# Attention and feed-forward on one core: a second tile of six sequences, first products in halves, weight splitting on GpSimd

## The chip, the cores and the metric

One core of one Trainium2 chip. The metric is device time in microseconds of one execution. The engines are TensorE (PE, its weight loads PEld), VectorE (DVE), ScalarE (ACT), GpSimd (POOL) and SyncE (SP), which issues the transfers.

## What is computed

```python
B, H, S, D = (8, 8, 576, 64); stride = 32          # q, k, v in float32
scores = scale * np.matmul(q, k.transpose(0, 1, 3, 2))
mask_local = (rel >= 0) & (rel < stride)            # heads 0 to 3
mask_strided = (rel >= 0) & (pos[None, :] % stride == pos[:, None] % stride)   # heads 4 to 7
attn = softmax(np.where(masks, scores, -1e9))
x = np.matmul(attn, v).transpose(0, 2, 1, 3).reshape(B * S, H * D)    # 4608 x 512
h = x @ w_in                                        # 512 x 2048
g = 0.5 * h * (1.0 + erf(h * inv_sqrt2))
return g @ w_out                                    # 2048 x 512
```

## The kernel before

The 4608 tokens are taken in 12 tiles of 384. A tile is a list of 12 strided rows of 32 tokens; the table `VISITS` says in which order the rows (r0 to r1 of a sequence b) are taken. For each tile 16 feed-forward steps follow, one for each block of 128 hidden channels, 192 in all. Step n makes `H_n` (`ffn_h`, 12 first products of 384 columns, for four channel blocks c of x: c 0 and 1 come from the local heads, 2 and 3 from the strided ones), then gelu, a high part `gh` and a low part `gl` (`ffn_g`), and then adds to the output banks (`ffn_o`, 9 second products of 512 columns). Every operand is a pair of a high part and a low part, so that three products stand for one.

Attention lies between these steps. The local heads are "jobs" L0 to L35, three to a tile, whose scores and values are small products of TensorE. The strided heads are computed by VectorE, unit by unit (at most 4 rows of a visit), one multiply-and-sum of 64 channels for each pair of a row and an earlier row, and one accumulation for each pair again; only tile 0's strided heads go over TensorE (`half_tile` a and b, `strided_tile` A). Once a tile, at step 13 of the tile, `visit` issues the value products of the next tile's jobs and the scores of the tile after that, 144 small products in a row; below this is a tile change.

The weights come as packed 64-bit words, one load of 1 MB for each of 16 blocks (`load_w`, at most three on their way). `split_w` makes the pair of parts of a block f in five operations: `lead` (the top 16 bits, L154 or L156), the upper halves `other` (L159), a merge with a shift (L161), the high part (L165 or L167) and the low part (L169). These, the first three local jobs, tile 0's strided heads, steps 0 to 15 of the feed-forward (`f0` to `f15`) and the strided unit jobs of tile 1 (`u1`) are issued in an order written out by hand, the list `START`, one word for one piece of a job: `w` loads a weight, `c` splits it, `q` and `v` load a local job's inputs, `L` runs it, `S` and `B` load tile 0's strided inputs. Each engine runs its own instructions in this order. After it, `step` places the steps, the tile changes and the strided operations by a rule of shares.

Of the kernel before, what the change touches and what calls it, by code (L numbers as in the profile page):

```python
# [10 lines left out]
F32 = mybir.dt.float32  # L11
# [13 lines left out]
P = 128  # L25
# [13 lines left out]
VISITS = [(0, 0, 12), (1, 0, 4), (2, 0, 4), (3, 0, 4), (4, 0, 18), (5, 0, 18), (6, 0, 18), (7, 0, 18),  # L39
          (1, 4, 18), (2, 4, 18), (3, 4, 18), (0, 12, 18)]  # L40
# [8 lines left out]
    q0 q2 S0 q1 v0 w0 B0 w1 L0 w3 L2 L0 L0 L2 L2 L0 a0 L0 L0 b0 a0 L2 a0 L0 L2 a0 L1 L2 b0 b0 b0 L0 L1  # L49
    L2 a0 L0 b0 a0 L1 b0 a0 b0 w2 a0 b0 a0 q5 b0 L0 a0 v2 L1 L2 b0 L0 v1 c0 L1 a0 q4 L1 b0 c0 L1 A0 L1  # L50
    c0 A0 w5 A0 c1 c0 A0 c0 c1 A0 c3 L5 c1 c3 L2 L5 L1 c2 v5 c1 w6 L4 c3 w4 L1 L2 c2 L1 L2 L4 f0 L5 w7
    c2 L4 c1 c2 f0 f1 L5 c2 f0 c5 f0 L4 c5 f0 c3 f1 c5 f1 f2 c4 f1 c4 c5 c3 f1 f2 f2 c4 c7 L5 f2 c4 c5
    f3 L5 w8 c7 c4 w9 E f2 f3 L5 c6 f3 c7 c6 f4 f3 c7 c6 w12 f3 c7 f4 f4 c8 c6 f5 w10 f4 c8 v3 c6 q3 w11
    c9 c8 f4 f5 u1 f5 c9 f6 f5 w13 u1 c8 v4 c9 f5 c12 w15 c8 f6 e f6 f7 c12 u1 c9 f6 c12 f6 f7 f7 c9 w14
    c10 f8 f7 c12 u1 c10 c12 f7 f8 c10 c11 f9 u1 c11 c10 f8 c13 c11 L4 L3 f9 f8 f9 c10 f8 c13 f9 c11 c13
    f10 c14 c11 c14 L3 f9 c13 f10 c14 f10 L4 f11 u1 f10 c13 L3 f10 L4 u1 f11 L3 f12 u1 f11 c14 f11 u1
    f13 f12 f12 c15 c14 f11 f13 f12 f13 u1 c15 f14 f13 u1 f12 f14 c15 f14 f14 c15 L3 u1 f13 L3 c15 u1 L3
# [3 lines left out]
TOP_V = [6]  # L61
HIGH_V = [0, 1, 2, 3, 5, 6, 10, 13]
QUOT_V = (0, 1)
# [3 lines left out]
def units(most):  # L67

    res = []
    for k, (vi, b, r) in enumerate(ROWS):  # L70
        if res and res[-1][0] == vi and k % TR and res[-1][3] < most:
            res[-1][3] += 1
        else:
            res.append([vi, b, r, 1, k // TR, k % TR])
    return res
# [7 lines left out]
def attn_ffn_kernel(ctx: ExitStack, tc: tile.TileContext, qk, vl, qka, va, qs, ks, vs, w, out):  # L83
# [30 lines left out]
    smask = const.tile([P, MA], F32, name="smask")  # L114
    mask = const.tile([P, LK], F32, name="mask")
    mask0 = const.tile([P, LK], F32, name="mask0")

    bmask = {i: const.tile([P, 2 * STRIDE], F32, name=f"bmask{i}") for i in (None, 0, 1)}
# [22 lines left out]
    def split_w(f):  # L141
# [9 lines left out]
        lead = lpool.tile([P, 2 * DM], F16, name=f"lead_{f}", tag="lead", bufs=1)  # L151
# [7 lines left out]
        nc.scalar.activation(other.bitcast(I32), lead.bitcast(I16), AF.Copy, scale=65536.0)  # L159
# [11 lines left out]
        w2[f] = wt[:, :, DM:]  # L171

# [109 lines left out]
    def band_job(x, bt, sx=None):  # L282
# [25 lines left out]
        msk = bmask[first_[0] if first_ else None]  # L308
# [150 lines left out]
    def load_strided(gr, nm):  # L459

        if gr is None:
            return
        src = {"q": qs, "k": ks, "v": vs}[nm]
        t = spool.tile([P, NR, D], F32, name=f"s{nm}_{gr}", tag=f"s{nm}", bufs=1)
        for vi in first_of[gr]:
            b, r0, r1 = VISITS[vi]
            o = groups[vi][1]
            sq[vi, nm] = t[:, o:o + r1]
            if nm != "q":
                r0 = 0  # L470
            nc.sync.dma_start(t[:, o + r0:o + r1], src[b, :, r0:r1])
# [8 lines left out]
    def strided_qk(u):  # L480
        vi, _, r0, nr, t, k = PLACE[u]
        W = r0 + nr
# [7 lines left out]
        for c in range(W):  # L490
            for r in range(max(0, c - r0), nr):
                def f(r=r, c=c):
                    junk = spool.tile([P, D], F32, name=f"junk_{u}_{r}_{c}", tag="junk", bufs=4)
                    nc.vector.tensor_tensor_reduce(  # L494
                        junk, sq[vi, "q"][:, r0 + r, :], sq[vi, "k"][:, c, :], 1.0, 0.0,
                        ALU.mult, ALU.add, ss[u][:, r, c:c + 1])
                ops.append((0.137, f))
# [10 lines left out]
    def strided_av(u):  # L508
        vi, _, r0, nr, t, k = PLACE[u]
        W = r0 + nr  # L510
# [17 lines left out]
        for c in range(W):  # L528
            for r in range(max(0, c - r0), nr):
                def f(r=r, c=c):  # L530
                    acc = ss[u, "acc"]
                    wgt = ss[u][:, r, c:c + 1]
                    if c == 0:
                        nc.vector.tensor_scalar_mul(acc[:, r, :], sq[vi, "v"][:, c, :], wgt)
                    else:
                        nc.vector.scalar_tensor_tensor(  # L536
                            acc[:, r, :], sq[vi, "v"][:, c, :], wgt, acc[:, r, :], ALU.mult, ALU.add)
                ops.append((0.196, f))
# [16 lines left out]
    def alternate(us, what, first):  # L555
# [7 lines left out]
        for ops in zip(*todo):  # L563
# [4 lines left out]
            for u, x in zip(us, ops):  # L568
                r0, nr = PLACE[u][2:4]
                key = [r for c in range(r0 + nr) for r in range(max(0, c - r0), nr)]  # L570
                rows_ += [[f for k, f in zip(key, x) if k == r] for r in range(nr)]
# [377 lines left out]
```

## Time and profile before

| what | value |
|---|---|
| median of 3 runs | 876.04 us (874.67 to 878.77) |
| the profiled execution | 877.5 us, span 875.7 us |
| TensorE busy | 856.4 us of the span |
| VectorE, ScalarE, GpSimd busy | 706.2, 482.7, 17.5 us |
| transfers | 66.67 MB, 76 GB/s in the mean |

The span runs from the first to the last instruction. Busy times of TensorE are modelled, since products overlap; the distance from one product to the next says more than the length of one.

### The profile page before, as it was taken

What the parts mean: (1) busy time and instruction counts of PE and PEld (TensorE: products, weight loads), DVE (VectorE), ACT (ScalarE), POOL (GpSimd) and SP (SyncE); (2) the same over time, 40 slices, a digit from 0 to 9 for tenths busy, and PEclk for the clock granted to TensorE, in tenths of its full rate; (3) what the DMA queues carried; (4) which work ended last, traced back from release to release, by engine and by line L of the source; (5) the groups of instructions that cost most, each with busy time, mean ns of one, the idle gap of its engine ahead of it and who ended that gap; (6) DMA issues with size and microseconds to landing.
All of it is one profiled execution on the core that took longest, in us unless ns stands there. A gap on an engine that the chain in (4) does not pass through costs nothing.

```text
span 875.7 us, 19634 instructions
## 1 busy us (share of the span) xinstructions
PE 856.4 (98%) x6082; PEld 771.0 (88%) x6082; DVE 706.2 (81%) x4901; ACT 482.7 (55%) x1001; POOL 17.5 (2%) x89
## 2 busy tenths in 40 slices
PE   5999999999999999999999999999999989999998
PEld 4888898999999999999999899989989979989997
DVE  6998999998989997889999979899799993751111
ACT  7888585566465375357355445556547435443222
POOL 5000100000000000000000000000000000000000
PEclk9799999999999999999999999999999999999999
DMA  9695301320310320310311121131032002000001
GB/s 352 223 380 200 115 24 37 108 76 8 128 47 9 101 97 10 104 44 8 97 50 58 55 76 47 34 122 48 9 101 80 12 30 59 18 6 12 26 1 37
DMA packets 34552, 66.67 MB, mean 76 GB/s; under 512 B 6800, under 2 KB 16528, under 8 KB 34448
## 3 DMA queue, kind: packets, MB, share of 16 engines
q1 hardware_dynamic: 34448, 65.43, 22.1%
q8 instruction: 48, 0.79, 0.4%
q14 instruction: 56, 0.46, 0.2%
HBM read 51.64 MB, written 9.44 MB: 70 GB/s over the span
## 4 chain that ended last, share of the span: by engine, by line
PE 90%; DVE 3%; DMA 3%; ACT 2%; SPq 1%; issue 1%; DVEq 0%; ACTq 0%
PE H L619 15%; PE O L659 14%; PE O L660 14%; PE H L621 14%; PE H L620 14%; PE O L658 14%; PE X_L L337 1%; PE S L297 1%; DMA ws<-in_w_dram 1%; DMA qka<-in_qka_dram 1%; DMA sk<-in_ks_dram 1%; DVE ws L161 1%; SPq L326 1%; PE S L337 1%; DVE w L169 1%
## 5 line engine op out<-in xcount | busy, mean ns | idle before, releaser
L628 ACT ACTIVATE H<-H 128x384 f32<-128x384 f32 x192 | 91.3, 476 | 363.0 <-PE H L621 304.3
L619 PE MATMUL H<-xh,w 128*128 128x384 f32 x768 | 261.6, 341 | 1.5 <-DVE gl L632 1.4
L621 PE MATMUL H<-xh,w 128*128 128x384 f32 x768 | 260.6, 339 | 0.0
L620 PE MATMUL H<-xl,w 128*128 128x384 f32 x768 | 259.4, 338 | 0.4 <-DVE xl L238 0.4
L536 DVE SCALAR_TENSOR_TENSOR acc<-sv,sc,acc 128x64 f32<-128x64 f32 x1158 | 249.5, 275 | 0.7
L660 PE MATMUL O<-w,gl 128*128 128x512 f32 x576 | 228.3, 396 | 0.0
L659 PE MATMUL O<-w,gh 128*128 128x512 f32 x576 | 227.7, 395 | 0.0
L658 PE MATMUL O<-w,gh 128*128 128x512 f32 x576 | 224.4, 390 | 0.0
L494 DVE CUSTOM_DVE_ANT_0 junk<-sq,sk 128x64 f32<-128x64 f32 x1290 | 203.8, 217 | 3.5 <-DMA sk<-in_ks_dram 2.4
L632 DVE TENSOR_TENSOR gl<-H,gh 128x384 fp32r<-128x384 f32 x192 | 105.7, 551 | 106.0 <-ACT gh L630 105.1
L619 PEld LDWEIGHTS H<-xh,w 128*128 128x128 f32 x768 | 145.4, 189 | 11.1 <-DVE gl L632 1.7
L620 PEld LDWEIGHTS H<-xl,w 128*128 128x128 f32 x768 | 145.3, 189 | 8.5 <-DVE xl L238 0.8
L621 PEld LDWEIGHTS H<-xh,w 128*128 128x128 f32 x768 | 145.0, 189 | 0.1
L660 PEld LDWEIGHTS O<-w,gl 128*128 128x128 f32 x576 | 108.1, 188 | 23.7 <-DVE gl L632 0.6
L659 PEld LDWEIGHTS O<-w,gh 128*128 128x128 f32 x576 | 108.1, 188 | 18.2
L658 PEld LDWEIGHTS O<-w,gh 128*128 128x128 f32 x576 | 108.5, 188 | 17.3
L494 DVE DVE_READ_ACCUMULATOR2_ANT sc<- 128x1 f32 x1290 | 103.6, 80 | 0.0
L630 ACT CAST gh<-H 128x384 fp32r<-128x384 f32 x192 | 92.2, 480 | 6.1
L628 ACT ACT_TABLE_LOAD x60 | 77.0, 1283 | 1.0
L504 ACT ACT_TABLE_LOAD x35 | 44.9, 1283 | 0.6
L315 ACT ACTIVATE PT_L<-P_L,nm_L 128x64 f32<-128x64 f32 x132 | 44.2, 337 | 0.3
L315 ACT ACT_TABLE_LOAD x24 | 30.8, 1283 | 0.5
(114 smaller groups left out, 488.7 us busy)
## 6 DMA issues: line engine op xcount, KB each, us to landing
ws<-in_w_dram SPq DMA_DIRECT2D x16, 1023.8 KB, 10.1
qk<-in_qk_dram SPq DMA_DIRECT2D x36, 320.0 KB, 5.0
out_dram<-ob SPq DMA_DIRECT2D x34, 256.0 KB, 2.4
vl<-in_vl_dram SPq DMA_DIRECT2D x36, 192.0 KB, 4.3
sk<-in_ks_dram SPq DMA_DIRECT2D x8, 576.0 KB, 5.5
sv<-in_vs_dram SPq DMA_DIRECT2D x8, 576.0 KB, 3.9
band<-PT_L SPq DMA_DIRECT2D x240, 16.0 KB, 1.8
sq<-in_qs_dram SPq DMA_DIRECT2D x4, 576.0 KB, 4.4
```

Source lines behind the costliest of these rows:

```text
L315: nc.scalar.activation(pv[:, :, h, :], p1[:, h * 2 * QB:(h + 1) * 2 * QB].rearrange("p (c t) -> p c t", c=2), AF.Exp, bias=nm[:, h:h + 1], ...
L494: nc.vector.tensor_tensor_reduce(junk, sq[vi, "q"][:, r0 + r, :], sq[vi, "k"][:, c, :], 1.0, 0.0, ALU.mult, ALU.add, ss[u][:, r, c:c + 1])
L536: nc.vector.scalar_tensor_tensor(acc[:, r, :], sq[vi, "v"][:, c, :], wgt, acc[:, r, :], ALU.mult, ALU.add)
L619: nc.tensor.matmul(hp, w1[f][:, 0, c, :], xh[:, c, :], start=(c == 0), stop=False)
L620: nc.tensor.matmul(hp, w1[f][:, 0, c, :], xl[:, c, :], start=False, stop=False)
L621: nc.tensor.matmul(hp, w1[f][:, 1, c, :], xh[:, c, :], start=False, stop=(c == NC - 1))
L628: nc.scalar.activation(hp, hp, AF.Gelu)
L630: nc.scalar.copy(gh, hp)
L632: nc.vector.tensor_tensor(gl, hp, gh.bitcast(F32), ALU.subtract)
L658: nc.tensor.matmul(o, gh[:, sl], w2[f][:, 0, :], start=(f == 0), stop=False)
L659: nc.tensor.matmul(o, gh[:, sl], w2[f][:, 1, :], start=False, stop=False)
L660: nc.tensor.matmul(o, gl[:, sl], w2[f][:, 0, :], start=False, stop=(f == NF - 1))
```

## The change

The order of the rows is another: tile 1 now holds two rows of each of six sequences, and the rest of these sequences follows in one visit each. A unit may now hold rows of several sequences, and one load brings the six sequences. Steps 0 and 1 make their first products in two halves of the channel blocks; step 0 begins with the local half, step 1 with the strided half. Seven of the upper halves and eight of the high parts go to GpSimd. `lead` has two buffers. The lead-in products at the very start go from 49 to 28. Masks and zeros lie in the `pbig` buffer. The scores for tiles 4 and 9 are issued two steps after the tile change instead of in it. `START` is another list, and GpSimd's work in it is now in the written order too.

```diff
-VISITS = [(0, 0, 12), (1, 0, 4), (2, 0, 4), (3, 0, 4), (4, 0, 18), (5, 0, 18), (6, 0, 18), (7, 0, 18),
-          (1, 4, 18), (2, 4, 18), (3, 4, 18), (0, 12, 18)]
+VISITS = [(0, 0, 12), *[(b, 0, 2) for b in range(1, 7)], (7, 0, 18), *[(b, 2, 18) for b in range(1, 7)],
+          (0, 12, 18)]
...
-    q0 q2 S0 q1 v0 w0 B0 w1 L0 w3 L2 L0 L0 L2 L2 L0 a0 L0 L0 b0 a0 L2 a0 L0 L2 a0 L1 L2 b0 b0 b0 L0 L1
+    q2 q0 q1 S0 w0 w1 v2 v0 L2 B0 v1 L0 L2 w4 L1 L2 L0 L0 L1 L2 b0 L2 L1 L2 L0 a0 b0 L0 b0 L0 L1 b0 L1
...
-TOP_V = [6]
-HIGH_V = [0, 1, 2, 3, 5, 6, 10, 13]
-QUOT_V = (0, 1)
+TOP_V = [5, 6]
+HIGH_V = [2]
+
+WORD_P = [0, 4, 6, 8, 11, 12, 14]
+HIGH_P = [0, 1, 3, 4, 5, 6, 7, 8]
+QUOT_V = (1, 2)
+
+HALVES = {0: ((0, 1), (2, 3)), 1: ((2, 3), (0, 1))}
...
-        lead = lpool.tile([P, 2 * DM], F16, name=f"lead_{f}", tag="lead", bufs=1)
+        lead = lpool.tile([P, 2 * DM], F16, name=f"lead_{f}", tag="lead", bufs=2)
...
-        nc.scalar.activation(other.bitcast(I32), lead.bitcast(I16), AF.Copy, scale=65536.0)
+        if f in WORD_P:
+            nc.gpsimd.tensor_scalar(other.bitcast(I32), lead.bitcast(I16), 65536.0, None, ALU.mult)
+        else:
+            nc.scalar.activation(other.bitcast(I32), lead.bitcast(I16), AF.Copy, scale=65536.0)
...
+        elif f in HIGH_P:
+            nc.gpsimd.tensor_copy(wt[:, 0, :], hf)
...
-    def ffn_h(n):
+    def ffn_h(n, parts=None):
+
         t, f = divmod(n, NF)
         xh, xl = xt[t]
-        hp = ps_h.tile([P, TT], F32, name=f"H_{n}", tag="H")
-        for c in range(NC):
...
+        hp = hps[n] = ps_h.tile([P, TT], F32, name=f"H_{n}", tag="H")
+        parts = parts or (range(NC),)
+        for cs in parts:
+            for c in cs:
+                nc.tensor.matmul(hp, w1[f][:, 0, c, :], xh[:, c, :], start=(c == parts[0][0]), stop=False)
...
+            yield
...
-    for i in range(49):
+    for i in range(28):
...
-    with tc.manual_schedule(engines={ET.DVE, ET.Activation, ET.PE, ET.SP}):
+    with tc.manual_schedule(engines={ET.DVE, ET.Activation, ET.PE, ET.SP, ET.Pool}):
...
-    FIRST, VISIT = 2, 13
+    FIRST, VISIT, LATE = 2, 13, (4, 9)
...
-    score_at = {ready[1] + FIRST: 2, **{n: t + 1 for n, t in value_at.items()}}
+    score_at = {ready[1] + FIRST: 2, **{n + 2 * (t + 1 in LATE): t + 1 for n, t in value_at.items()}}
```

The written order decides what each engine does next. On VectorE, before, from the merge of weight block 0 (`ws_0`) to the maxima of job 5 (`xl_0` is the low part of tile 0's x, `w_0` the split weight):

```order
L161 SCALAR_TENSOR_TENSOR ws_0_305<-ws_0_305 128x1024
L435 STREAM_TRANSPOSE qka_0_297<-A0_0_357 128x256
...
L165 CAST w_0_596<-ws_0_305 128x1024
L169 TENSOR_TENSOR w_0_596<-ws_0_305,w_0_596 128x1024
L441 TENSOR_TENSOR xl_0_494<-qka_0_297,xh_0_493 128x4x48 x4
L161 SCALAR_TENSOR_TENSOR ws_1_308<-ws_1_308 128x1024
L311 ISA P_L5_638,nm_L5_640<-S0_1_610,bmask0_90 128x64
```

The same stretch of VectorE's list in the change:

```order
L174 SCALAR_TENSOR_TENSOR ws_0_281<-ws_0_281 128x1024
...
L433 TENSOR_TENSOR va_0_278<-va_0_278,Az_0_0_459 128x8x24
L261 TENSOR_TENSOR xl_0_505<-S0_L0_307,xh_0_504 128x2x128
...
L184 TENSOR_TENSOR w_0_492<-ws_0_281,w_0_492 128x1024
L261 TENSOR_TENSOR xl_0_505<-S0_L1_326,xh_0_504 128x2x128
L174 SCALAR_TENSOR_TENSOR ws_1_283<-ws_1_283 128x1024
L458 STREAM_TRANSPOSE qka_0_277<-A0_0_396 128x256
...
L184 TENSOR_TENSOR w_1_610<-ws_1_283,w_1_610 128x1024
L464 TENSOR_TENSOR xl_0_505<-qka_0_277,xh_0_504 128x4x48 x4
```

The high parts (L165) are gone from it, the local `xl` stand ahead of the strided ones, and the maxima of a band job stand behind the stretch.

On GpSimd, in the change, behind the masks and memsets of the start (`lead` is a weight's top 16 bits, `ws` its packed words, `w` the split weight):

```order
L759 MEMSET bmask2_88 32x32 x2
L170 TENSOR_SCALAR ws_0_281<-lead_0_446 128x1024
L180 CAST w_0_492<-ws_0_281 128x1024
L180 CAST w_1_610<-ws_1_283 128x1024
L170 TENSOR_SCALAR ws_4_324<-lead_4_612 128x1024
L180 CAST w_4_661<-ws_4_324 128x1024
L180 CAST w_3_758<-ws_3_469 128x1024
L170 TENSOR_SCALAR ws_6_600<-lead_6_771 128x1024
L180 CAST w_5_881<-ws_5_648 128x1024
```

Before, the memsets of the score buffers of the strided units stood here, and no operation on weights.

## Rows read from the trace of the kernel before

**Rows 1.** The page, busy time, share of the span and instructions.

```profile
PE 856.4 (98%) x6082; PEld 771.0 (88%) x6082; DVE 706.2 (81%) x4901; ACT 482.7 (55%) x1001; POOL 17.5 (2%) x89
```

**Rows 2.** Timeline of TensorE: start us, length us, line, operands, [idle before <-releaser].

```profile
8.53 1.92 PE L387 MATMUL A<-qka 64*32 64x24 f32 x128 [1.79 <-DMA qka<-in_qka_dram]
...
26.53 0.69 PE L619 MATMUL H<-xh,w 128*128 128x384 f32 x1
27.61 0.69 PE L620 MATMUL H<-xl,w 128*128 128x384 f32 x1 [0.39 <-DVE xl L238]
...
33.98 0.39 PE L658 MATMUL O<-w,gh 128*128 128x512 f32 x1
...
49.44 0.33 PE L619 MATMUL H<-xh,w 128*128 128x384 f32 x1
...
53.63 0.33 PE L619 MATMUL H<-xh,w 128*128 128x384 f32 x1
```

**Rows 3.** The chain that ended last, around tile changes: start us, us, what.

```profile
642.04 1.08 PE X_L L337 x32
...
711.88 1.08 PE X_L L337 x32
...
714.50 2.94 issue
...
786.49 1.08 PE X_L L337 x32
```

**Rows 4.** Stretches: length, busy us (xcount) of PE, PEld, DVE, ACT, POOL, clock, DMA, GB/s.

```profile
0.00:20.00 20.00, 12.26 (x434) 10.43 (x434) 11.73 (x59) 13.50 (x42) 11.03 (x54) 0.97 0.92 362
29.00:31.00 2.00, 2.00 (x8) 2.00 (x8) 2.00 (x4) 1.98 (x9) 0.00 (x0) 0.50 1.01 410
33.00:35.00 2.00, 2.00 (x12) 1.83 (x11) 1.90 (x7) 1.97 (x3) 0.00 (x0) 1.00 0.72 279
```

**Rows 5.** Who waited for whom: us in total, times, longest us.

```profile
PE H L619 <- DVE gl L632: 1.4, 1, 1.4
```

**Rows 6.** Timeline of ScalarE near 74 us.

```profile
74.44 1.10 ACT L156 CAST lead<-ws 128x1024 f16<-128x1024 bf16 x1 [2.38 <-DMA ws<-in_w_dram]
```

**Rows 7.** Groups by line and shape: busy us, mean ns | idle before us.

```profile
L161 DVE SCALAR_TENSOR_TENSOR ws<-ws 128x1024 uint32<-128x1024 uint32 x16 | 19.5, 1221 | 4.2 <-ACT ws L159 4.0
L169 DVE TENSOR_TENSOR w<-ws,w 128x1024 fp32r<-128x1024 f32 x16 | 19.3, 1212 | 0.0
...
L165 DVE CAST w<-ws 128x1024 fp32r<-128x1024 f32 x8 | 5.4, 678 | 0.0
...
L159 ACT ACTIVATE ws<-lead 128x1024 int32<-128x1024 int16 x16 | 18.3, 1143 | 0.2
...
L814 POOL MEMSET band<- 128x2048 f32 x1 | 1.8, 1811 | 2.6 <-DVE w L169 2.6
...
L726 POOL COPY mask<-mask 128x64 f32<-128x64 f32 x1 | 0.2, 237 | 0.1
```

**Rows 8.** Timelines of GpSimd and of VectorE, first 30 us.

```profile
4.18 0.26 POOL L724 TENSOR_SCALAR_AFFINE_SELECT mask<-mask 64x96 f32<-64x96 f32 x1
...
6.04 0.26 DVE L211 CUSTOM_DVE_ANT_0 pbig<-S_L,mask 128x96 f32<-128x96 f32 x1 [3.96 <-POOL mask L726]
...
21.77 1.69 DVE L441 TENSOR_TENSOR xl<-qka,xh 128x192 fp32r<-128x192 f32 x4
```

**Rows 9.** The page, DMA queues: packets, MB, share of 16 engines.

```profile
q8 instruction: 48, 0.79, 0.4%
```

**Rows 10.** Stretches from the start to two tile changes, columns as in rows 4.

```profile
0.00:362.63 362.63, 350.08 (x2737) 313.93 (x2737) 328.05 (x2170) 238.74 (x473) 15.10 (x72) 0.98 0.33 116
...
0.00:711.80 711.80, 699.25 (x5137) 629.44 (x5137) 648.10 (x4637) 424.81 (x874) 17.48 (x89) 0.99 0.26 88
```

**Rows 11.** Two like operations of VectorE, grouped by line and shape.

```profile
L400 DVE TENSOR_TENSOR va<-va,Am 128x192 f32<-128x192 f32 x2 | 0.8, 382 | 0.0
...
L410 DVE TENSOR_TENSOR va<-va,Az 128x192 f32<-128x192 f32 x2 | 0.6, 350 | 0.0
```

More of the change, by code (lines that the diff above doesn't have):

```diff
@@ L70, in units, with pairs @@
     for k, (vi, b, r) in enumerate(ROWS):
-        if res and res[-1][0] == vi and k % TR and res[-1][3] < most:
+        n = VISITS[vi][2] if VISITS[vi][1] == 0 and VISITS[vi][2] <= most // 2 else 0
+        if res and k % TR and res[-1][3] < most and (res[-1][0] == vi or n and res[-1][6] == n):
             res[-1][3] += 1
         else:
-            res.append([vi, b, r, 1, k // TR, k % TR])
-    return res
+            res.append([vi, b, r, 1, k // TR, k % TR, n])
+    return [(*x[:6], x[6] or x[3]) for x in res]
+def pairs(u):
+    _, _, r0, nr, _, _, per = PLACE[u]
+    return [(c, r) for c in range(r0 + per) for r in range(nr) if r0 + r % per >= c]
 PLACE = units(UR)
@@ L113, in attn_ffn_kernel @@
     ident = const.tile([P, P], F32, name="ident")
[L114 to L118, printed above, removed]
+    bmask = {i: const.tile([P, 2 * STRIDE], F32, name=f"bmask{len(i)}") for i in ((), (0,), (0, 1))}
     def rows(j):
@@ L171, in split_w @@
         w2[f] = wt[:, :, DM:]
+    pbig = slot("pbig", [P, 4 * DM])
+    rest = [pbig[:, i * 2 * DM + 4 * LK + DM:(i + 1) * 2 * DM] for i in range(2)]
+    pbig = [pbig[:, i * 2 * DM:(i + 1) * 2 * DM] for i in range(2)]
+    mask, mask0 = [r[:, 0:LK] for r in rest]
+    smask, zero = rest[0][:, LK:LK + MA], rest[1][:, LK:LK + 32]
     xt = {}
@@ L307, in band_job @@
         first_ = [a for a in range(2) if LPLACE[2 * x + a][1] == 0]
-        msk = bmask[first_[0] if first_ else None]
+        msk = bmask[tuple(first_)]
         for h in range(HL):
@@ L489, in strided_qk, with f @@
         ops.append((0.0, init))
[L490 to L497, printed above, removed]
+        for c, r in pairs(u):
+            def f(r=r, c=c):
+                junk = spool.tile([P, D], F32, name=f"junk_{u}_{r}_{c}", tag="junk", bufs=4)
+                nc.vector.tensor_tensor_reduce(
+                    junk, sq[vi, "q"][:, r0 + r, :], sq[vi, "k"][:, r // per * per + c, :], 1.0, 0.0,
+                    ALU.mult, ALU.add, ss[u][:, r, c:c + 1])
+            ops.append((0.137, f))
         def sm():
@@ L735, in attn_ffn_kernel @@
                                     fill=NEG, base=-1, channel_multiplier=-1)
-            if i is not None and g == 2 * i:
+            if g % 2 == 0 and g // 2 in i:
                 nc.gpsimd.memset(m[sl, 0:STRIDE], NEG)
@@ L749, in ffn @@
     def ffn(n):
-        ffn_h(n)
-        yield
+        yield from ffn_h(n, HALVES.get(n))
         yield from ffn_g(n)
@@ L831, in visit @@
         t = value_at.get(n, 0)
-        if score_at.get(n, 0):
-            banks[score_at[n]] = score_banks(score_at[n])
+        new = t + 1 if t else score_at.get(n, 0)
+        if new and new not in banks:
+            banks[new] = score_banks(new)
         for i in range(JPT if t else 0):
@@ L855, in step @@
         if NB <= n < NS:
-            ffn_h(n)
+            for _ in ffn_h(n):
+                pass
             for _ in ffn_g(n):
```

80 lines of the change are left out of this document (37 added, 43 removed).

## The prediction

> **What bounds the kernel now.** Read the page's first part first: TensorE is busy 98% of the span and VectorE 81% [rows 1]. A busy TensorE is not yet a bound, so the next question is whether it runs at its own pace. In TensorE's timeline two neighbouring steps begin at 49.44 and 53.63 us [rows 2]: 4.19 us for the 12 first and 9 second products of one step. 192 such steps are 804 us. The chain of waits shows the second regular cost: attention's products at a tile change make the period from one change to the next 69.84 us (642.04 to 711.88) [rows 3], that is 16 steps of 4.19 (67.0) and 2.8 us. From the first feed-forward product on, TensorE's work is therefore fixed, and the change leaves it as it is. What can be won lies in three places, and the reader should find each of them.
>
> First, the start. The first product of step 0 begins at 26.53 us, and the second products of step 0 at 33.98 [rows 2]. [...]
> Second, one wait of TensorE for VectorE's `gl`, 1.4 us [rows 5]; behind it stands ScalarE, which waited 2.38 us, until 74.44, for a late weight to land [rows 6].
> Third, one tile change went wrong: the chain has 2.94 us of "issue" at 714.50, and the next change comes at 786.49 [rows 3], 74.61 us after the one before instead of 69.84. Step 173 has the cheaper change without new scores, but its own cost falls behind 786.49, so 4.77 us is the price of the wait and of the slower clock behind it.
>
> **The start, step by step.** What decides is VectorE's list. Before, its list runs without a pause from the first merge of `w0` (the L161 operation, ready when ScalarE's L159 has made the upper halves) until 27.6 us: TensorE still waited 0.39 us for the last `xl` at 27.61 [rows 2]. The list is about 10.1 us long, so it began near 17.5. In the change the same stretch, merge of `w0` to the last `xl`, holds: two merges 2.3 and two low parts 2.3 (1.22 and 1.21 each, some 0.07 less in a row) [rows 7], the four `xl` of the strided heads 1.7 [rows 8], and by the same kind of timeline rows four transposes 1.4, three `xl` of the local heads 1.2, four operations of the second half of the strided softmax 0.9 and a copy 0.35. That is 10.1 us again: the two high parts that leave VectorE (0.68 each [rows 7]), a third merge and a block of four maxima (3.1 us in all) make room for work that stood ahead of it. So the list gets no shorter; it starts earlier.
>
> How much earlier: local job 2 is now first, and it needs `mask`, not `mask0`. GpSimd ends `mask` at 4.44 us; VectorE waited for `mask0` until 6.04 [rows 8]. The gain of 1.6 us is eaten for the strided tile, since its inputs land behind a third 320 KB load: TensorE began on them at 8.53 [rows 2]; at 362 GB/s [rows 4] the extra load is 0.9 us, so 9.4. From there: half of the 1.92 us of scores 1.0, three VectorE operations 1.1, the exponential 0.35, then ScalarE makes `lead` of `w0` (1.10, the row's form [rows 6]) until 13.0. The upper halves are now GpSimd's, an operation that no row of before shows. GpSimd's memset of 2048 elements takes 1.81 us and its copy of 64 takes 0.24 [rows 7]: 0.88 ns an element and about 0.2 fixed, 1.1 us for 1024. The least it can be is VectorE's 0.68, and if reading and writing add up, 0.2 + 2 x 0.9 = 2.0 us. I take 1.2, near the first slope, since the operation has one input. VectorE then merges at about 14.5, and 10.1 us later, with some 0.4 of hand-overs, the second half of step 0 can start: **25.0 us**. GpSimd's high part of `w0` is hidden behind 2.0 us of VectorE's list, that of `w1` behind the 1.4 us of transposes; at 2.0 us a piece the chain grows by 0.8 + 0.6 and the half starts at 26.4.
>
> The first half of step 0 (6 of 24 products) is done by then: it needs only the local heads and `w0`, which the same list gives near 19.5. From 25.0 on 18 products remain, 0.32 us each at the low clock (24 took 26.53 to 33.98), and one block of 0.7 us of scores: 31.5 instead of 33.98, **2.5 us won**. I let the clock rise where it did before, some 6 us into dense work. Were it high at once, VectorE would hold the second product of step 2: merges of `w4` and `w2`, maxima, low part of `w4`, high part of `w2`, `gl`, low part of `w2`, 6.3 us after 25.0. So no more than 3.7 can be won; with slow GpSimd operations it is 1.1, and less if the loads lag.
>
> **The rest of the weights.** GpSimd takes 7 upper halves and 8 high parts; VectorE loses 7 x 0.68 = 4.8 us and gets one `lead` more, ScalarE loses 7 x 1.14 and one high part [rows 7]. Tile 1 of six sequences by two rows has 18 products and 18 accumulations where three by four had 30 each, another 4 us off VectorE before step 16; the 12 come back later in the same total, where VectorE's work is done long before TensorE's. From step 2 on I find slack at each weight: low part of `w3` near 36 for a product due at 38, of `w5` near 45 for 47, more after that. So the 1.4 us of [rows 5] should go: **1.4**, nothing at worst. The scores of tiles 4 and 9 move two steps on; each adds one return to feed-forward products, 0.1 us: **-0.2**. Loads merged into one issue, later stores in two pieces and four more units with their handful of small operations lie under TensorE's work.
>
> **The wait at 714 us.** The page's queue 8 carries instructions, 48 packets of 0.79 MB in all [rows 9]: 16.4 KB each. TensorE's 12,164 products and weight loads in 48 packets are about 253 to a packet. A step uses 42 instructions in 4.19 us, a tile change 288 (144 products and their loads) in 2.7 us, more than one packet. I read the wait as TensorE out of instructions: "issue" says that it waited for nothing else. From change to change the two counts grow by 480 each (2737 at 362.63, 5137 at 711.80, five changes) [rows 10], with 12 queue waits that the views leave out 972: each change begins 52 places earlier in its packet of 256. Counting the stalled change as place 0, the others stand at 4, 52, 56, 104, 108, 156, 160 and 208, and wait for nothing. The 21 lead-in products that go are two passes of product and load each, 84 instructions; in the built order the changes come 88 earlier. Their places are then 17, 20, 69, 72, 121, 170, 173, and two at -31 and -34; those at 17 and 20 are the split ones, 104 instructions only. None is near 0; the two lie between -48 (208, passed) and 0 (stalled). I take the whole **4.8** as won and give a new wait three chances in ten.
> [...]
>
> **Sum.** 2.5 + 1.4 - 0.2 + 4.8 = 8.5 us. The profiled execution took 877.5, 1.5 more than the median of 876.04. Taken off the one this gives 869.0, off the other 867.5. I say **868.5**.
>
> **The rivals.**
> *The instruction wait stays or moves to another change*: 868.5 + 4.8 = 873.3. For it: two changes come within 34 places of the bad one. Against: eight of nine passed.
> *The earlier half product does not bring step 1 forward*: GpSimd at 2.0 us or more and loads that arrive later (the values now stand behind two weights) put the second half at 27.5, nothing won at the start: 871.0.
> *GpSimd and VectorE stand in each other's way*, the slower side. Five GpSimd operations stand in a row in the chain to the first `gl` (upper halves and high parts of `w0`, then the high part of `w1`, then both of `w4`, whose low part stands ahead of `gl` in VectorE's list). Each us more on one delays the second products of step 0 by five. To end over 880.4 all 8.5 us and 4.4 more must be lost: 12.9/5 = 2.6 us more, 3.8 us for an operation. Then the time is 881 or above. For it: VectorE is near 100% busy there, with two inputs in most operations. Against: while GpSimd ran its selections, VectorE's L400 took 0.38 us and the like L410, with GpSimd still, 0.35 [rows 11]: 9% more, not a doubling.
> [...]
>
> **How the numbers follow.** The forecast has 0.52, the instruction wait 0.21, the unchanged start 0.18, the slow side 0.09. A difference under 0.5% (871.7 to 880.4) is about what a measurement of this kernel cannot tell from no change. The forecast lies below it nearly whole, the unchanged start on the line and somewhat more than half below: faster 0.62; the wait and the rest: same 0.29; slower 0.09. Alone the forecast runs from 865.5 (3.7 at the start, the higher gain elsewhere and the lower of the two bases) to 871. The range takes in the wait and half of its start lost, 865 to 876.
>
> **What would show it.** In the profile after: first feed-forward product near 19.5, second products of step 0 near 31.5; GpSimd's 1024-element operations near 1.2 us; no idle time over 1 us on TensorE after 32; no "issue" wait at a tile change, and all changes about 69.8 apart but for the two split ones. Wrong would be GpSimd operations over 2 us, VectorE's merges waiting for them, or "issue" again near 292 or 642.

## The result, and the profile after

The change takes 880.5 us in the median of 22 runs (877.49 to 883.23), the kernel before 876.52 in 22 runs beside it (873.26 to 881.45). The ratio is 1.0042, with an interval of 1.0031 to 1.0054: slower by 0.4%, where 0.9% faster was forecast. The time lies outside the range given. The profiled execution took 880.4 us, its span is 878.4.

The page of the change answers to [rows 1] and [rows 9]; the columns are the same.

```profile
PE 859.5 (98%) x6040; PEld 771.1 (88%) x6040; DVE 712.3 (81%) x4919; ACT 487.5 (55%) x1008; POOL 51.6 (6%) x107
q8 instruction: 47, 0.77, 0.4%
```

The shares say nothing: 98% and 81% as before. What moved is seen by cutting the execution at three places of TensorE's work. Both kernels were profiled three times, and each entry is the mean, with the three values behind it (us from the span's start, from the trace).

| | before | the change | difference of the stretch |
|---|---|---|---|
| second products of step 0 end | 36.2 (36.2, 36.5, 35.9) | 37.9 (38.9, 38.0, 36.9) | +1.7 |
| of step 16 | 111.8 (111.3, 111.5, 112.5) | 116.2 (116.4, 115.2, 116.9) | +2.7 |
| of step 191, the last | 871.5 (871.9, 870.0, 872.6) | 873.9 (874.2, 873.0, 874.6) | -2.0 |
| device time | 877.1 (877.5, 875.7, 878.2) | 880.1 (880.4, 879.4, 880.5) | +0.5 |

So the loss is made in two stretches of the start, 4.4 us in all, and half of it is won back later. In these profiles the whole is 3.0 us, in the medians 4.0; the single executions spread by 6 to 8 us, and the profiles show some of what they differ in (waits of TensorE in the first 35 us that come in one execution and not in the next).

**Step 0.** TensorE's timeline of the change, first profile (columns: start, duration, instruction). It answers to [rows 2].

```profile
23.06 1.97 PE L453 MATMUL A<-va 24*32 24x64 f32 x128
24.95 0.69 PE L645 MATMUL H<-xh,w 128*128 128x384 f32 x1
...
27.78 0.69 PE L645 MATMUL H<-xh,w 128*128 128x384 f32 x1
30.09 0.69 PE L646 MATMUL H<-xl,w 128*128 128x384 f32 x1 [1.62 <-DVE xl L464]
...
36.01 0.45 PE L645 MATMUL H<-xh,w 128*128 128x384 f32 x1
36.30 0.33 PE L646 MATMUL H<-xl,w 128*128 128x384 f32 x1
36.48 0.33 PE L647 MATMUL H<-xh,w 128*128 128x384 f32 x1
36.65 0.39 PE L684 MATMUL O<-w,gh 128*128 128x512 f32 x1
```

The first half of step 0 begins at 24.95 (19.5 was forecast) and the second half stands for the last `xl` until 30.09 (25.0). The distance between neighbouring first products is 0.32 us until 36.0 and 0.17 behind it, so the slow pace lasts to 36, where before it lasted to 32.6; in the other two profiles of the change it ends at 31 and 32. The second products begin at 36.65, not at 31.5.

**What made the last `xl` late** stands in the timelines of GpSimd (first fence) and VectorE (second) of the same profile; the bracket is the idle time before an instruction and what ended it.

```profile
15.41 2.83 POOL L170 TENSOR_SCALAR ws<-lead 128x1024 int32<-128x1024 int16 x1 [2.10 <-ACT lead L166]
19.57 1.10 POOL L180 CAST w<-ws 128x1024 fp32r<-128x1024 f32 x1 [1.32 <-DVE ws L174]
25.20 1.15 POOL L180 CAST w<-ws 128x1024 fp32r<-128x1024 f32 x1 [4.53 <-DVE ws L174]
26.31 2.88 POOL L170 TENSOR_SCALAR ws<-lead 128x1024 int32<-128x1024 int16 x1
```

```profile
14.67 0.17 DVE L429 TENSOR_SCALAR Az<-Az 128x8 f32<-128x8 f32 x1
...
18.27 1.23 DVE L174 SCALAR_TENSOR_TENSOR ws<-ws 128x1024 uint32<-128x1024 uint32 x1 [1.26 <-POOL ws L170]
...
19.80 0.91 DVE L429 TENSOR_SCALAR Az<-Az 128x8 f32<-128x8 f32 x1
...
22.46 1.21 DVE L184 TENSOR_TENSOR w<-ws,w 128x1024 fp32r<-128x1024 f32 x1
...
26.41 2.02 DVE L184 TENSOR_TENSOR w<-ws,w 128x1024 fp32r<-128x1024 f32 x1
28.36 1.68 DVE L464 TENSOR_TENSOR xl<-qka,xh 128x192 fp32r<-128x192 f32 x4
```

The operation that no row of before showed, GpSimd's upper halves, takes 2.83 us, and the first merge stands 1.26 us for it. And the two engines hold each other up: VectorE's operation on 8 elements a lane takes 0.17 us at 14.67, and 0.91 at 19.80, where it ends with GpSimd's cast (19.57 to 20.67); the low part takes 1.21 us alone, and 2.02 where it starts 0.1 us behind GpSimd's next operation.

**Steps 1 to 16.** TensorE's longest wait of the whole execution, from its waits (us in total, times, longest), and then VectorE's timeline just before it:

```profile
PE H L647 <- DVE w L184: 2.8, 1, 2.8
```

```profile
80.04 0.22 DVE L519 CUSTOM_DVE_ANT_0 junk<-sq,sk 128x64 f32<-128x64 f32 x1 [2.70 <-DMA sk<-in_ks_dram]
...
81.22 1.22 DVE L184 TENSOR_TENSOR w<-ws,w 128x1024 fp32r<-128x1024 f32 x1
```

VectorE stands 2.70 us for `sk`, the strided k of the next group, and the low part of block 11 is queued behind the eight operations that need it. TensorE waits 2.81 us at 82.49 for that low part (1.9 and 3.4 in the other two profiles). `sk` was issued at 71.28: 24 transfers of a band job, some 0.6 us each to issue, and four weights stood ahead of it in SyncE's queue. The wait of 1.4 us for `gl` [rows 5] did go; this one came in its place, twice as long. Steps 10 to 15, where both waits lie, take 2.4 of the 2.7 us.

**After step 16** the wait at the tile change [rows 3] is in all three profiles of the kernel before, at the same product, and in none of the change. The second profile of before, TensorE's timeline:

```profile
712.79 0.64 PE L337 MATMUL S<-band,vl 96*64 96x64 f32 x16
713.35 1.14 PE L297 MATMUL S<-qk 64*32 64x64 f32 x92
717.16 0.30 PE L297 MATMUL S<-qk 64*32 64x64 f32 x4 [2.67 <-issue]
```

It is 2.94, 2.67 and 2.67 us long, and with the slower products behind it (0.32 us apart at 719 to 721 us in the first profile, at a granted clock of 0.50) that tile change costs 4.8, 3.0 and 4.5 us more than its neighbours. That it is a wait for instructions the trace shows directly: in the first profile TensorE stops at 714.50, a packet starts on queue 8 at 714.91 and has landed at 715.94, and TensorE goes on at 717.44. Against these 4.1 us the later stretch is only 2.0 shorter, since the change has small waits of its own: the two tile changes at places -31 and -34 cost 0.7 and 0.4 us more than the others in the first profile, each of the two split changes costs 0.2 (0.1 was forecast), and two steps in which the second products stand for the copies of the output take 4.53.

### The profile page after: what moved, and what is told of

Read it like the earlier page. It is cut to its first block, busy times and chain, and to the rows that moved or that the text cites. A ratio compares the mean times of both kernels' runs of the same rounds, so it can differ in the third digit from the quotient of the medians.

```text
span 878.4 us, 19594 instructions
## 1 busy us (share of the span) xinstructions
PE 859.5 (98%) x6040; PEld 771.1 (88%) x6040; DVE 712.3 (81%) x4919; ACT 487.5 (55%) x1008; POOL 51.6 (6%) x107
## 4 chain that ended last, share of the span: by engine, by line
PE 90%; DMA 6%; ACT 1%; DVE 1%; SPq 1%; issue 1%; ACTq 0%; DVEq 0%
PE H L645 15%; PE H L647 14%; PE O L686 14%; PE H L646 14%; PE O L685 14%; PE O L684 14%; DMA ws<-in_w_dram 5%; PE S L320 1%; PE X_L L360 1%; DMA sk<-in_ks_dram 1%; ACT PT_L L338 1%; PE S L360 1%; ACT L338 0%; DVE ws L174 0%; DVE junk L519 0%
## 5 line engine op out<-in xcount | busy, mean ns | idle before, releaser
L513 POOL MEMSET sc<- 128x64 f32 (+7 forms) x40 | 5.1, 129 | 627.6 <-DVE acc L561 627.3
```

## The experiments

Each kernel ran beside the kernel before on the same chip. The third column is the ratio to it with its interval; the change itself stands at 1.0042.

| run | median us | ratio | O_0 end | O_16 end | O_16 to O_191 |
|---|---|---|---|---|---|
| 1 before, 28 lead-in | 877.59 | 1.0003 [0.9989, 1.0018] | 37.1 | 112.4 | 760.2 |
| 2 change, 49 lead-in | 885.48 | 1.0100 [1.0078, 1.0123] | 36.5 | 118.7 | 760.4 |
| 3 change, upper halves on ScalarE | 882.95 | 1.0066 [1.0043, 1.0088] | 37.9 | 116.6 | 758.0 |
| 4 change, no weights on GpSimd | 882.54 | 1.0065 [1.0043, 1.0087] | 39.9 | 120.8 | 757.2 |
| 5 change, values first | 881.94 | 1.0049 [1.0029, 1.0069] | 36.5 | 114.4 | 757.8 |
| 6 change, strided load early | 879.82 | 1.0030 [1.0011, 1.0049] | 37.7 | 114.7 | 757.6 |
| 7 change, four edits | 878.41 | 1.0002 [0.9984, 1.0020] | 37.7 | 116.3 | 756.9 |
| 8 before, 24 lead-in | 885.27 | 1.0079 [1.0050, 1.0109] | 46.7 | 121.4 | 761.2 |
| 9 before, 51 lead-in | 874.32 | 0.9954 [0.9938, 0.9970] | 37.3 | 113.7 | 755.7 |
| 10 change, 51 lead-in, strided load early | 879.37 | 1.0010 [0.9991, 1.0028] | 38.9 | 117.1 | 756.8 |
| 11 change without halves | 881.28 | 1.0038 [1.0016, 1.0059] | 37.6 | 117.5 | 757.3 |
| 12 change, first two weights off GpSimd | 882.02 | 1.0049 [1.0030, 1.0068] | 37.3 | 118.1 | 756.9 |
| 13 change, all limits | 878.85 | 1.0026 [1.0015, 1.0038] | 39.0 | 117.0 | 756.9 |

The last three columns (us) are from the one profile of each and give where the second products of steps 0 and 16 end, and the stretch from there to step 191; a profile can lie up to 3.6 us off its median.

**Lead-in products, where instructions run out (1, 2, 8, 9).** Every lead-in product taken away moves all tile changes by four instructions in their packets: for 21 of them the page of the change has 6040 products and as many loads, where before had 6082 of each.

```diff
-    for i in range(49):
+    for i in range(28):     # run 1; 24 in run 8, 51 in run 9
```

> The kernel before with 28 lead-in products instead of 49, nothing else. Theory of packets: the 84 instructions less move every tile change 84 places earlier in its packet; the stalled one at place 0 goes to 172, one (of 52) to -32 and one (of 56) to -28. The kernel of the change showed 0.74 and 0.38 us in the steps at -31 and -34, so about 4.8 - 1.3 = 3.5 us faster than before, near 873.0, no wait over 1 us at a tile change. Rival, the wait at 714 us is no matter of packets but of that place in the program: no difference, 876.5.

Missed in the median, which is where the rival put it. Its profile is the slowest of twelve executions, 2.2 us over their median. In it the wait at 714 is gone (step 157 takes 6.93 us, the normal length of a tile change), but the start is 1 us later, and TensorE waits 2.55 us for `gl` at 657, behind VectorE, which stood 2.13 us at 650 for the strided values to land; counted with the products behind it that is 4.3 us. In this profile, what was won in one place was lost in two.

The change with the 49 lead-in products of before:

> The change with 49 lead-in products again, nothing else. Theory of packets: all changes come 84 places later than in the change, so the ones at 173 and 170 come to 1 and -2, beside place 0 that stalled in the kernel before, and those at -31 and -34 come clear: two waits of about 4.8 us each in place of 1.1 in all, at the tile changes near 370 and 720 us; 8.5 us slower than the change, near 889. Rival, packets play no part: 880.5.

The direction held, about 5 us slower than the change. There are waits with no releaser at the two tile changes that stand at places 1 and -2, 1.40 us at 374.69 and 1.45 at 726.2; counted with the products behind them these changes cost 1.8 us each more than the others, where 4.8 was expected. The rest is mostly the wait for block 11, 5.99 us here.

> The kernel before with 24 lead-in products instead of 49: 100 instructions of TensorE fewer, so that the nine tile changes stand at places 60, 8, -44, 160, 108, 56, 4, -48 and 156 of the packet; none is where a wait was seen (0) and none between -40 and 2. If the wait for instructions at 714 us, 4.77 us in the profiled execution, is in most executions of the kernel before, the time is 872 to 873.5. If it is in few of them, or if what the earlier finish gains is taken by a late strided load as in the kernel before with 28 lead-in products (2.55 us at 657), the time is 876 to 877.5.

Neither: it is 8 us slower, and in its profile, the slowest of six executions and 3 us over their median, 10.5 us are lost by the end of step 0. TensorE's timeline of its start, and three waits with no releaser in a row:

```profile
16.33 0.74 PE L254 MATMUL S_L<-qk 64*64 64x96 f32 x5 [2.32 <-issue]
...
22.03 1.50 PE L430 MATMUL A<-va 24*32 24x64 f32 x93
28.44 0.71 PE L430 MATMUL A<-va 24*32 24x64 f32 x35 [4.91 <-issue]
...
35.64 0.66 PE L297 MATMUL S<-qk 64*32 64x64 f32 x18 [2.45 <-issue]
```

Nothing but the number of lead-in products differs. Counted in TensorE's record, the first two stand at instructions 451 and 706. In the other profiles the waits of this kind in the first 35 us stand at 450, 706 and 961 or 962, 256 apart (12,164 products and loads and 151 queue waits in the trace of before, over 48 packets, are 257 to a packet); two, the third one here (908) and one of run 13 (1052), stand elsewhere. Counted the same way the wait at 714 us stands at 10,690 and those of run 2 at 5827 and 10,690, again whole multiples of 256 from 450, give or take one. In run 8 a packet begins to come over queue 8 at 13.84 and at 25.90 us, 0.2 us before TensorE stops and 2.4 us after it has; in run 1 the first comes at 9.3. In front of these places stand the small products of attention, 93 of them and their loads in 1.5 us. So the wait of the tile change exists in the start too. This profile has one more at a tile change, 1.08 us at 586.04. By the counting of the prediction it stands at place 4, and the kernel before has a change at that place too, at 362.6, without a wait in three profiles; so the place isn't all that decides.

> The kernel before with 51 lead-in products instead of 49: eight more instructions of TensorE, at a time when it waits for the first load anyway, so the start stays. The tile changes move eight places on in their packets: the one that stood at place 0 stands at 8, the others at 12, 60, 64, 112, 116, 164, 168 and -40. If the wait at 714 us is TensorE out of instructions and hangs on that place, step 157 takes 6.93 us, steps 0 to 16 are as before (step 16 ends at 111 to 112.5), and the time is 3 to 4.5 us lower: 873. If the wait hangs on something else at that point of the program, it stays, and the time is 877.

Met in the time and at the tile change, and it is the fastest kernel of the study, under both. The same place as in the fence above, in its profile:

```profile
715.17 0.66 PE L337 MATMUL S<-band,vl 96*64 96x64 f32 x16
715.76 1.17 PE L297 MATMUL S<-qk 64*32 64x64 f32 x96
716.86 0.44 PE L619 MATMUL H<-xh,w 128*128 128x384 f32 x1
```

The 96 score products run through, and from step 16 on it takes 755.7 us where the three profiles of before take 760.5, 758.6 and 760.1. The start did not move by design; in this profile late loads make it 1.2 to 2.4 us later than before's.

**GpSimd (3, 4, 12).** Run 3 gives GpSimd no upper halves, run 4 no weights at all, run 12 none of block 0 and no high part of block 1.

```diff
-WORD_P = [0, 4, 6, 8, 11, 12, 14]      # runs 3 and 4: []; run 12: [4, 6, 8, 11, 12, 14]
-HIGH_P = [0, 1, 3, 4, 5, 6, 7, 8]      # run 4: [], with HIGH_V as before; run 12: [3, 4, 5, 6, 7, 8]
```

> The change with the seven upper halves back on ScalarE; the high parts stay on GpSimd. Theory of GpSimd's price: its upper halves took 2.8 to 3.8 us where ScalarE takes 1.14, and the first stands in the chain to step 0, so the second half of step 0 comes 1.5 to 2 us earlier; the later part of the start, which waits for loads, gives back little: 1.5 to 2.5 us faster than the change, near 878.5. Rival, the start is bound by the loads alone (values behind two weights): no difference, 880.5.

> The change with no weight operation on GpSimd: upper halves on ScalarE, high parts divided between VectorE and ScalarE as in the kernel before; order and loads of the change. Theory that GpSimd's own time and its holding up of VectorE cost most of the start: VectorE's long forms (2.0 us instead of 1.2) go, it gets 4.8 us of high parts back; 2 to 4 us faster than the change, 876.5 to 878.5. Rival, GpSimd relieves VectorE and the loads cost the time: 0 to 3 us slower than the change, 880.5 to 883.5.

Both times the rival: no gain (the profile of run 4 is the slowest of six executions, 2.7 us over their median). In run 3 VectorE's list begins 1.5 to 2.7 us earlier than in the change and does not end earlier, since it now waits for ScalarE's `xh` and for TensorE:

```profile
15.54 1.23 DVE L174 SCALAR_TENSOR_TENSOR ws<-ws 128x1024 uint32<-128x1024 uint32 x1 [0.17 <-ACT ws L172]
...
20.64 0.42 DVE L261 TENSOR_TENSOR xl<-S_L,xh 128x256 fp32r<-128x256 f32 x1 [1.99 <-ACT xh L259]
...
26.23 1.44 DVE L458 STREAM_TRANSPOSE qka<-A 128x256 f32<-128x256 f32 x4 [1.39 <-PE A L453]
...
28.70 1.67 DVE L464 TENSOR_TENSOR xl<-qka,xh 128x192 fp32r<-128x192 f32 x4
```

Yet the price of GpSimd on VectorE is in the groups by form, first the change (GpSimd's upper halves and high parts, VectorE's merges and low parts), then run 4:

```profile
L170 POOL TENSOR_SCALAR ws<-lead 128x1024 int32<-128x1024 int16 x7 | 23.4, 3336 | 17.2 <-ACT lead L166 15.0 <-DMA first<-PT_L 1.6 <-DVE lead L164 0.6
L180 POOL CAST w<-ws 128x1024 fp32r<-128x1024 f32 x8 | 10.8, 1353 | 22.8 <-DVE ws L174 14.1 <-issue 8.7
...
L174 DVE SCALAR_TENSOR_TENSOR ws<-ws 128x1024 uint32<-128x1024 uint32 x16 | 21.9, 1374 | 5.0 <-POOL ws L170 2.8 <-POOL sc L513 2.2
L184 DVE TENSOR_TENSOR w<-ws,w 128x1024 fp32r<-128x1024 f32 x16 | 21.2, 1328 | 0.8 <-POOL w L180 0.5 <-ACT w L182 0.3
```

```profile
L184 DVE TENSOR_TENSOR w<-ws,w 128x1024 fp32r<-128x1024 f32 x16 | 19.4, 1222 | 0.7 <-ACT w L182 0.7
L174 DVE SCALAR_TENSOR_TENSOR ws<-ws 128x1024 uint32<-128x1024 uint32 x16 | 19.4, 1219 | 3.0 <-ACT ws L172 3.0
```

With GpSimd quiet the two forms are back at the 1.22 and 1.21 us of [rows 7]; beside it they are 4.3 us longer in 32 operations. VectorE has seven high parts of 0.68 less in exchange, 4.8 us, so the two about cancel.

> The change with the upper halves of block 0 and the high parts of blocks 0 and 1 on ScalarE instead of GpSimd; the other weights stay on GpSimd. In the change's profiles GpSimd's upper half takes 2.83 us where ScalarE's takes 1.14, and two operations of VectorE in the list to the last xl are 0.75 and 0.85 us longer while GpSimd runs. First theory (these three, 3.3 us, are most of what the second half of step 0 is late): the last xl is ready 2 to 3 us earlier than in the change, 26 to 28 instead of 28.7 to 30.5, the second products of step 0 end at 35 to 36.5, the time is 878 to 879. Rival (loads and TensorE's own waits set it: values that land at 18 to 21, instructions): the last xl moves by less than 1 us and the time is 880 to 882.

The rival, and it says why. The first merge stands at 15.22 us (18.27 in the change), but the last `xl` ends at 29.8. Waits of VectorE (first fence) and of TensorE (second) from 10 to 32 and to 35 us:

```profile
DVE qka L458 <- PE A L453: 2.5, 1, 2.5
DVE xl L261 <- ACT xh L259: 1.1, 1, 1.1
```

```profile
PE S_L L292 <- DMA vl<-in_vl_dram: 2.4, 2, 1.7
PE A L453 <- issue: 2.2, 1, 2.2
```

With GpSimd out of the chain, TensorE stands for the local values (2.4) and for instructions (2.2, the 706th), and VectorE's transposes wait 2.5 us for it.

**Loads (5, 6).** Run 5 reorders the first loads, run 6 issues the strided q and k (`E`) earlier; the engines' own orders stay.

```diff
-    q2 q0 q1 S0 w0 w1 v2 v0 L2 B0 v1 L0 L2 w4 ...
+    q2 q0 S0 q1 v2 v0 w0 B0 v1 w1 L2 L0 L2 w4 ...          # run 5
-    ... w12 c8 w11 w13 f5 ... w15 c10 f8 E c11 f8 ...
+    ... w12 c8 w11 w13 E f5 ... w15 c10 f8 c11 f8 ...      # run 6
```

> The change, with only the order of its first ten loads altered: the strided inputs behind the second local job, the three local values ahead of the weights, the second weight last. No engine's own order changes. First theory (the start is late because its loads land late: qka at 11.04, the values at 18.3 to 21.3 us): values land by 12, qka by 9, TensorE's waits of 2.35 for qka and 1.35 for a value go, the second products of step 0 end near 36.5 instead of 38.89, step 16's near 114 instead of 116.42, the time is 2 to 3 us below the change's 880.5: 878. Rival (VectorE's list and the 2.8 us operation of GpSimd set the start, the loads are only the wait that comes last by the way): the second products of step 0 move by less than 1 us and the time stays 880 to 881.

The loads came as meant (`qka` at 6.86 instead of 11.04, the first two values at 8.7 and 9.5 instead of 18.3 and 19.2), and the waits for both are gone from its profile. The last `xl` still keeps TensorE until 29.10, since VectorE's first merge is held by GpSimd until 17.45. This profile is the fastest of twelve executions, 3.6 us under their median, so its early step 16 isn't typical. No gain in the median.

> The change, with only the load of the strided q and k of the next group issued right behind the weight of block 13 instead of behind that of block 15, so ahead of eight transfers of a band job. First theory (VectorE stands 3.2 us for sk until 80.04 with the low part of block 11 queued behind it, and TensorE waits 2.81 us for that): sk lands near 72, the wait of 2.81 goes, the second products of step 16 end near 113.7 instead of 116.42, the time is 2.5 us lower: 878. Rival (VectorE's list is late there for its own length): TensorE waits for another weight's part within ten us, the end of step 16 moves by less than 1 us and the time stays 880 to 881.

`sk` landed at 70.3, and VectorE's and TensorE's waits are gone, as the first theory said. The ratio is 1.0030 where the change's is 1.0042, some 1 us less and not 2.5, a difference that these runs cannot tell from none: TensorE waits 0.76, 0.39, 0.43 and 0.59 us elsewhere in the same stretch, for `gl`, a band and twice for `gh`.

**Several at once (7, 10, 13).** Run 7 joins 5 and 6 with blocks 0 and 4's upper halves on ScalarE and 25 lead-in products; run 10 joins 6 with 51; run 13 joins 10 with the values ahead of the weights, the first job's order kept, and no GpSimd work on blocks 0 and 1 nor in block 4's upper halves.

> The change with the loads of the start reordered, the strided load early, the upper halves of blocks 0 and 4 back on ScalarE, and 25 lead-in products instead of 28, which puts the nine tile changes at places 8, 60, -43, 161, 109, 57, 5, -46 and 158 of the instruction packet. First theory (loads, the late strided load and GpSimd's 2.8 us operations cost the time): step 16 ends near 111 as in the kernel before, nothing is lost at a tile change, the time is 873 to 875, under both kernels. Rival (the start is bound by VectorE's list): step 16 ends at 114 or later and the time is 877 or above.

The rival: level with the kernel before, 1.0002, which is clear of the change's interval, but its start is no better than the change's. `q1` now lands behind `S0` and TensorE waits 3.68 us for it, then 3.02 for instructions at the 450th.

> The change with 51 lead-in products instead of 28 and the strided load early. Its tile changes stand at 164, 112, 61, 9, -43, 161, 109, 58 and 6; none in the places where waits were seen (1, -2, -31, -34). If the number of lead-in products sets where TensorE runs out of instructions in the first 35 us (with 28 it did at the 450th or 706th instruction in most profiles of the change, with 49 at the 962nd), the second products of step 0 end near 36.5, step 16 near 113 and the time is 876 to 877.5. If the start is VectorE's, step 16 ends at 114.5 or later and the time is 879 to 881.

There is no wait for instructions in its profile at all, yet the second products of step 0 end at 38.9: 1.04 us of waiting for a job's inputs, 0.50 for `xl` and 1.28 for VectorE stand there instead, and the slow pace lasts to 36.5. The time is 879.4, as the rival said, though the ratio of 1.0010 is below the change's interval.

> The change with 51 lead-in products, the strided load of q and k early, the three local values loaded ahead of the first two weights, and no GpSimd operation on blocks 0 and 1 nor in the upper halves of block 4. If values, GpSimd and waits for instructions stand side by side and nothing else does, the last xl is ready at 25 to 26.5, the second products of step 0 end at 33.5 to 35.5 (36.9 to 38.9 in the change), step 16 near 110 to 112, and the time is 872.5 to 875. If TensorE's own chain through attention or VectorE's list is the bound whatever is taken away, the last xl stays at 27.5 or later and the time is 877 to 880.

The rival again. VectorE's waits from 8 to 31 us:

```profile
DVE xl L261 <- ACT xh L259: 1.9, 1, 1.9
```

ScalarE has taken over: it runs the upper halves and high parts that GpSimd had, and `lead` of block 1, which waits for its load until 19.98, stands ahead of the `xh` that VectorE needs.

**The halves (11).**

```diff
-HALVES = {0: ((0, 1), (2, 3)), 1: ((2, 3), (0, 1))}
+HALVES = {}          # and one f0 and one f1 fewer in START
```

> The change without the halves: steps 0 and 1 make their first products in one piece, behind the last xl, and one word of step 0 and one of step 1 are taken out of the written order. If the halves are worth what was forecast (6 of 24 products of step 0 done ahead of the last xl, 0.32 us each), the second products of step 0 end 1.5 to 2 us later than in the change's profiles (36.9 to 38.9) and the time is 882. If the first half only stands in front of a wait of 1.6 us for xl and the slow clock eats it, the second products of step 0 end within 0.7 us of the change's and the time is 880 to 881.

The second case: 37.6 without halves, 36.9 to 38.9 with them, and the same time. Without them the 24 products of steps 0 and 1 begin at 27.61 and stand once, for 0.68 us ahead of a block of scores; the pace is the higher one from 33.5 on. With them a pause of 0.8 to 1.6 us stands in the middle, and the slow pace lasts to 31, 32 and 36 in the three profiles.

**Two more profiles of each kernel**, for the table of stretches above:

> The kernel before, unchanged, profiled a second time: it tells whether the wait for instructions at 714 us belongs to the kernel or to one execution. If it belongs to the kernel, the step there (step 157) is again 10 us instead of 6.93 and the next one is longer too. If it belongs to the execution, as the kernel before with 24 or 28 lead-in products suggests (neither gained), step 157 is 6.93 here, or another tile change has the wait.

> The kernel before, unchanged, a third profile: as for the second. Three of three would say that the wait is the kernel's own; one or two of three that it comes and goes, so that what the change wins there is only a part of 4.77 us in the median.

> The change, unchanged, profiled a second time. Its first profile had no step longer than 5.01 us past step 16 but for tile changes, and step 16 ended at 116.42. First theory (the start costs the change 5 us, and the wait of 2.81 us for the weight of block 11 is the kernel's own): step 16 ends between 115.5 and 117.5 again and VectorE waits 3 us for sk again. Rival (the executions differ by waits for instructions in the crowded start and at tile changes): step 16's end differs by over 1.5 us, or a step past 16 is longer by 2 us or more.

> The change, unchanged, a third profile: as for the second. Three profiles with step 16 ending within 1.5 us of each other speak for the first theory, a spread above that for the rival.

The wait at 714 is the kernel's own, three of three. In the change step 16's end spreads by 1.7 us and the wait for block 11 is there each time; the second profile has 0.46 and 1.68 us without a releaser at instructions 450 and 706, the other two none. So both theories hold a part: 4.4 us is the change's own loss, and instructions add a spread to it.

## Why the prediction was wrong

- **The wait at 714 us** (4.8): right. It went, and its place in the packet matters (run 9 removes it with two lead-in products and nothing else, run 2 brings such waits back), though run 8 has one at a place that the kernel before passes. It is worth 4.1 us in the profiles and 3.2 in the median of run 9. An execution of before has 48 packets, and nineteen profiles together have 28 waits of TensorE without a releaser over 0.3 us, so most packets come without one; this one is 2.67 to 2.94 us long, behind 140 small products and their loads. The rows give 253 instructions to a packet; the 256 of the prediction is what the distance of the waits shows. What the forecast missed is the rest of that stretch: small waits at places -31 and -34, the splits and the output copies eat 2.1 of the 4.1.
- **The start** (2.5 won): the step that failed. The merge of block 0 was put at 14.5 and the second half of step 0 at 25.0. In the third profile of the change, whose loads came nearest to the forecast, the chain reads: GpSimd begins at 14.1, where `lead` was to end at 13.0; its operation takes 2.83 instead of 1.2; the list behind it 11.8 instead of 10.1, of which 0.73 is the operation on 8 elements and 0.82 the low part that stood beside GpSimd. Together 28.8. The 1.2 came from the slope of a memset and a copy of 64 elements (0.79 ns an element by these two rows, not 0.88) for an operation of another form (int16 in, int32 out), and even the upper bound of 2.0, reading and writing added, was too low. Two more parts of the step failed. The list doesn't start earlier: its first merge stands at 18.3, 17.3 and 17.0 us in the change and at 17.4, 17.7 and 17.2 before. And it isn't what decides alone: with the first upper halves on ScalarE and the loads as they were (runs 3, 4 and 12) the merge comes at 15.2 to 15.8, and the last `xl` still ends at 29.8 to 31.7, against 28.7 to 30.5 in the change, since VectorE then stands 1.1 to 2.5 us for `xh` and 1.4 to 2.5 for TensorE, which stood 2.4 to 3.2 for the values.
- **GpSimd and VectorE in each other's way** (the slower rival, 0.09): the waits are shown, their price was not what decided. The 9% of [rows 11] came from operations of 0.35 us beside short selections and misled; 0.17 us became 0.91 and 1.21 became 2.02. Beside casts the waits last about to the end of the cast: the 0.91 ends with it, and at 47.53 us a merge that starts 0.3 behind a cast takes 1.94 us and ends 1.09 behind it. Beside the upper halves the wait ends sooner, or there is none: the low part of 2.02 us ends at 28.43, 0.8 before the GpSimd operation that began ahead of it, so it did not wait for the whole of that one, and in the second profile a low part that starts 2.0 us behind the start of such an operation takes 1.18. But with GpSimd off all weights (run 4) the kernel is no faster, and GpSimd's high parts give VectorE back about what the waits take.
- **The unchanged start** (0.18): the second half came at 28.8 to 30.6, later than its 27.5, and the loss at step 0 is 1.7 us.
- **The slow clock**: "I let the clock rise where it did before, some 6 us into dense work" did not hold. The pace rose 6 us behind the first product of step 0 in the kernel before, and 11, 4.5 and 8 us behind it in the three profiles of the change, at 36, 31 and 32 us.
- **The wait of 1.4** ("nothing at worst"): the second step that failed, wrong by sign. It went, but the queue that SyncE works off was not followed behind 60 us: `sk` came late, and 1.9 to 3.4 us stand in its place.

So the start was put 3.9 us earlier and came 4.4 later. Which single part costs it can't be named: values, GpSimd, ScalarE and packets each stand in the chain, and taking one away (runs 5, 6, 11, 12) or most of them (13) left the time within 0.2% of the change's. Two combinations, runs 7 and 10, do come out 0.4 and 0.3% under it, clear of its interval; their profiles show 0.9 us of that behind step 16 (756.8 to 756.9 against 757.7) and none in the start, so where the rest comes from stays open. That the written order and the plan behind it are what costs the start, the one thing that no run undid, was only argued. Open too is the wait for the strided values at 650 to 667 us in runs 1 and 8, which run 9 doesn't show.

## What to carry to other kernels

Price an operation on an engine that hasn't run it by measuring it alone (GpSimd's upper halves took 2.83 us here where 1.2 was estimated), and price it twice: once for itself and once for what the engine that it holds up loses (here 4.3 us in 32 operations of VectorE). Where several engines' lists are balanced against each other, one part made faster can move the bound to its neighbour, as in run 12 to TensorE (2.5 us) and in run 13 to ScalarE (1.9 us); follow every queue, SyncE's too, to the end of the stretch. And look for waits without a releaser: here two extra products of eight columns, in a place that waits anyway, moved a burst of small products to another place in the packet and brought 3.2 us, where the whole change lost 4.0.

## What the hardware showed that was not expected

- GpSimd: upper halves of 1024 elements (16 bits in, 32 bits out, every second word) 2.83 us at best, 3.34 in the mean; its cast of 1024 elements 1.10 to 1.15 in six of eight in the change's first profile, 2.04 and 2.07 in the two that start 0.1 us behind the start of a merge or a low part of VectorE. ScalarE's same two forms take 1.15 and 1.13.
- Waits for instructions come 256 instructions apart in the crowded start as well, 0.5 to 4.9 us long, and depend on a few instructions more or less at the beginning of the program: run 8 has 9.7 us of them in the first 36 us, run 1, with four lead-in products more, none. Of the 28 waits of TensorE without a releaser over 0.3 us in the nineteen profiles, 26 stand a multiple of 256 instructions from the 450th, give or take one, and 25 end 1.3 to 1.5 us after a packet of queue 8 has landed.
- The granted clock of a record isn't always what the products ran at. In the change's first profile it is 1.00 from 25 us on, in the third 0.50, at the same 0.32 us from product to product (windows: stretch, busy time, instructions, granted clock, DMA share, GB/s; first profile, then third):

```profile
25.00:27.00 2.00, 2.00 (x8) 1.00 1.01 420
31.00:33.00 2.00, 2.00 (x8) 1.00 0.98 273
```

```profile
25.00:27.00 2.00, 2.00 (x36) 0.50 1.03 422
29.00:31.00 2.00, 2.00 (x7) 0.50 1.07 303
```
